# Second convolution with an fp32 first transform and its filter product kept in PSUM; layer-2 weights decoded earlier and passed through device memory

## The chip, the cores and the metric

One core of one Trainium2 chip runs the whole program. The metric is the device time of one execution in microseconds (us). Engine names in the profile: PE is TensorE (its matrix products), PEld its weight loads, DVE is VectorE, ACT is ScalarE, POOL is GpSimd, SP is the engine that issues most DMAs.

## What is computed

A spectral convolution along the sequence, then two gated layers. Cut from the reference:

```python
X = np.fft.rfft(x, axis=1)                      # x: 2 x 3008 x 256
y = np.fft.irfft(X * (filt_r + 1j * filt_i)[None], n=3008, axis=1)
x = y.reshape(6016, 256)
gate = 1.0 / (1.0 + np.exp(-(x @ w_gate)))      # layer 1, d_ff 1536; w_gate, w_val, w_out are float64
x = (gate * (x @ w_val)) @ w_out
h = x @ w_in                                    # layer 2, d_ff 2048; w_in, w_out are float64
out = (h * (1.0 / (1.0 + np.exp(-1.702 * h)))) @ w_out
```

## The kernel before, in words

**Products.** Most matrix products take operands of type fp32r. Each operand is split into a high part (an ACT copy to fp32r) and a low part (a subtraction, by `split`, L115), and `mm3` (L119 to L122) sums three products: high by high, high by low, low by high. One `mm3` is three matmuls. The layer products use a seven-product scheme on 2x2 blocks: seven `mm3` where eight would be needed.

**Stages.** The 6016 tokens are 12 tiles of 512 or 480 columns (`tiles`, six per sequence). The program runs: the convolution of sequence 0 in plain fp32 (methods `a0` to `d0`); layer 1 on tiles 0 and 1; then layer 1 on tiles 2 and 3 woven with the convolution of sequence 1 (the loop at L1004, below called the weave); layer 1 on the pairs of tiles p=2 to p=5 by the seven products (the loop at L1284); layer 2 on the pairs p=0 to p=5 (the loop at L1450). In the weave and after it the order on PE, ACT, DVE and POOL is the order in which the code emits instructions; SP's order is the emission order everywhere. Each engine works strictly through its own queue.

**The weave.** Its 20 passes k are 2 tiles by 10 blocks of 128 hidden units. In pass k the convolution unit j (16 channels, 16 units in all) is at five steps at once: `e1(k-5)`, `c1(k-1)`, `b1(k)`, `a1(k+1)`, `d1(k-2)`. `a1` splits the input into two parts (ACT, POOL); `b1` is the first transform (`mm3`) with a DVE transpose and a split; `c1` (L400) is the second transform, whose result in PSUM bank 7 is multiplied by the filter: `turn` (two ACT copies that swap real and imaginary halves into `v`; DVE `y = px * fr`, L414), `total` (DVE `v = v * fi`, L417, and `y = y + v`, L418), then the high part of `y` (ACT, L423) and its low part (DVE, L421); `d1` and `e1` are the third and fourth transforms, both in PSUM bank 6. Around them lie one pass of layer 1: two pairs of `mm3` into two of the banks 0 to 2 (`ring`), a sigmoid (L1030), the gate product on DVE (L1039), its split, and two `mm3` of an older block (`back`). In pass k the PE order is e1, c1, b1, d1, back, layer 1. `sign_f` (L278) spreads and signs the filter of one unit per pass. From k=12 on, DVE and ACT also prepare the operands of pair p=2 (`late_vec`, `late_act`).

**Layer 1, pairs.** A pass f of the loop at L1284 takes one hidden block: products x0, z1, back, y4, x5, back, back, x6, y2, back, x3 (the number is the operand's; the letter its PSUM bank). Between them DVE adds: z-add (L1360), y-add (L1369: it must read bank x before x6 adds to it), w-add (L1375: before x3 adds to it), and the gate products (L1381, L1390). `chore(n)` pops n steps of side work at four slots of a pass, whose sizes are `rate` (L1331): slot 0 lies between z-add and y-add on DVE's queue, slot 1 between y-add and w-add, slots 2 and 3 behind L1381.

**Side work.** The weights are float64 in memory: 512 KB (`load_raw`) hold a 128x512 block. `decode_steps` (L151) turns one into high and low fp32r parts: five DVE steps, two of ACT, a POOL subtraction. The 16 blocks (jobs) of layer 2 go to their final places (`slot`): five to `wl`, the rest over layer-1 weights as those are used up. Blocks 0 to 4 are decoded in p=3 and p=4, 5 to 11 in p=5, 12 to 15 in layer 2's p=0. `combine_w` (L1161) makes the four sums of two even-numbered weight blocks that the seven-product scheme needs: two in p=5, six in layer 2's p=0. Layer 2 waits in its pass fp until that pass is combined.

Of the kernel before, what the change touches and what calls it, by code (L numbers as in the profile page):

```python
# [87 lines left out]
def kernel(  # L88
# [23 lines left out]
    xscr = dram.tile([12, D, 512], F32, name="xscr")  # L112

# [104 lines left out]
    class Conv:  # L218
# [11 lines left out]
        def load_f(self, g):  # L230
            t = [self.ff.tile([P, 32, K1], F32, tag=f"f{i}", name=f"f{i}") for i in range(2)]
            gs = slice(g * 32, (g + 1) * 32)
            if self.b:
                for i in range(2):
                    nc.sync.dma_start(out=t[i][:64], in_=fd[i, :, gs])
            else:
                nc.sync.dma_start(out=t[0][:64], in_=fd[0, :, gs])
                for h in range(2):
                    hs = slice(g * 32 + h * 16, g * 32 + h * 16 + 16)
                    nc.sync.dma_start(out=t[1][h * 64:(h + 1) * 64, :16], in_=fd[1, :, hs])  # L240
            self.f[g] = t
# [158 lines left out]
        def c1(self, j):  # L400
            g, u = divmod(j, 2)
            px = ps[7][:, :384]
# [6 lines left out]
            y = self.fw.tile([P, 16, K1], F32, tag="y", name="y", bufs=1)  # L409
# [12 lines left out]

            return turn, total, lambda: nc.scalar.activation(out=yp[0], in_=y, func=AF.Copy), low  # L423
# [435 lines left out]
    sx0 = [w33.tile([P, PRE * 3, P], F32R, name=f"sx0{i}") for i in range(2)]  # L859
    pools = ExitStack()  # L860
# [11 lines left out]
    ring.remove(3)  # L872
# [121 lines left out]
    conv.sign_f(0, nc.gpsimd)  # L994
    conv.a1(0)
# [10 lines left out]
    for t in (2, 3):  # L1006
        for f in range(FK, FC1):
# [8 lines left out]
            if k + 1 < NCH:  # L1016
                conv.a1(k + 1)
# [40 lines left out]
            if k == 11:  # L1058
# [24 lines left out]
    ring.append(3)  # L1083
# [22 lines left out]
    fs.dst[3] = [packed(w, n) for w in xk]  # L1106


    def slot(j):
        if j < NWL:  # L1110
            return [w[:, j] for w in wl]
        return [w[:, j - NWL].rearrange("p v c m -> p (v c m)") for w in wg]

    NJ = FC2
    NEAR = 12
    done = set()
# [443 lines left out]
```

## Time and profile before

| | us |
|---|---|
| median of 3 runs (1247.91 to 1249.42) | 1248.92 |
| the profiled execution | 1249.48 |
| its span, first to last instruction | 1247.7 |
| PE busy in the span | 1169.2 |
| DVE, ACT, POOL busy | 762.7, 677.8, 546.8 |
| mean granted TensorE clock | 0.984 of 2.4 GHz |

A busy share is an average over stages that have different limits. In the rows, `<-` in a name stands between what is written and what is read; a bracket at the end of a row is the time that the engine sat idle before it and what ended that.

### The profile page before, as it was taken

How to read it: one execution, taken by the hardware profiler on the slowest of the kernel's cores; microseconds unless marked ns; L12 is line 12 of the kernel's file. 1: busy time of each engine (PE TensorE's matmuls, PEld its weight loads, DVE VectorE, ACT ScalarE, POOL GpSimd, SP SyncE). 2: the span in 40 equal slices, each digit the busy share in tenths (PEclk: the TensorE clock that was granted, in tenths of full speed). 3: DMA queues.
4: the chain of work that ended last, by engine and by line, in shares of the span. 5: the costliest groups of instructions: out<-in, count | busy, mean ns of one | idle time of the engine just before them, and what ended most of it. 6: DMA issues, size and time to landing. Idle time of an engine off the chain costs nothing.

```text
span 1247.7 us, 14513 instructions
## 1 busy us (share of the span) xinstructions
PE 1169.2 (94%) x4958; PEld 933.2 (75%) x4958; DVE 762.7 (61%) x1180; ACT 677.8 (54%) x1311; POOL 546.8 (44%) x426
## 2 busy tenths in 40 slices
PE   8999998787989999999998888899999999999998
PEld 4468876665767777878876675688888888888887
DVE  7899847898778876574578878742423324224211
ACT  5666526665445465454454555555655656556553
POOL 4800005665323354353353434554555545445443
PEclk9999998999989999999999999999999999999999
DMA  8564402332130011020012102001010010010000
GB/s 203 130 207 158 102 18 72 86 88 72 26 114 1 1 59 60 1 90 13 1 51 85 51 18 68 18 1 68 1 59 9 1 66 1 27 42 2 34 1 32
DMA packets 36011, 66.55 MB, mean 53 GB/s; under 512 B 3648, under 2 KB 12480, under 8 KB 35936
## 3 DMA queue, kind: packets, MB, share of 16 engines
q1 hardware_dynamic: 33968, 62.45, 17.0%
q10 hardware_dynamic: 1968, 3.17, 0.8%
q8 instruction: 39, 0.64, 0.2%
q14 instruction: 36, 0.29, 0.1%
HBM read 45.02 MB, written 19.79 MB: 52 GB/s over the span
## 4 chain that ended last, share of the span: by engine, by line
PE 50%; DVE 4%; issue 4%; POOL 2%; ACT 1%; ACTq 0%; DVEq 0%; POOLq 0%
PE ps L120 17%; PE ps L121 17%; PE ps L122 16%; DVE ps L1369 1%; DVE m L161 1%; POOL g L1415 1%; POOL wg L180 1%; DVE ps L1360 0%; POOL wo L1415 0%; DVE sg L1381 0%; DVE ex L156 0%; ACT sg L1379 0%; DVE wv L1169 0%; POOL g L117 0%; DVE yp L940 0%
## 5 line engine op out<-in xcount | busy, mean ns | idle before, releaser
L117 POOL TENSOR_TENSOR g<-sg,g 128x512 fp32r<-128x512 f32 (+1 forms) x116 | 155.7, 1350 | 269.6 <-ACT g L116 226.0
L1415 POOL TENSOR_TENSOR g<-sg,g 128x512 fp32r<-128x512 f32 (+1 forms) x128 | 167.2, 1321 | 160.7 <-ACT sg L1412 134.5
L120 PE MATMUL ps<-yp,wg 128*128 128x512 f32 (+1 forms) x373 | 147.5, 396 | 0.9 <-ACT wg L177 0.9
L121 PE MATMUL ps<-yp,wg 128*128 128x512 f32 (+1 forms) x373 | 146.3, 392 | 0.8 <-DVE yp L117 0.8
L122 PE MATMUL ps<-yp,wg 128*128 128x512 f32 (+1 forms) x373 | 145.4, 391 | 0.0
L1486 DVE TENSOR_TENSOR ps<-ps,s 128x512 f32<-128x512 f32 (+1 forms) x48 | 32.9, 686 | 153.1 <-PE ps L122 151.0
L1415 POOL TENSOR_TENSOR wo<-sg,wo 128x512 fp32r<-128x512 f32 (+1 forms) x64 | 83.1, 1307 | 83.6 <-ACT sg L1412 76.1
L1412 ACT ACTIVATE sg<-ps 128x512 f32<-128x512 f32 (+1 forms) x192 | 114.3, 595 | 0.0
L120 PE MATMUL ps<-g,wo 128*128 128x512 f32 (+1 forms) x288 | 113.1, 393 | 0.3 <-ACT wo L177 0.3
L121 PE MATMUL ps<-g,wo 128*128 128x512 f32 (+1 forms) x288 | 113.2, 393 | 0.0
L122 PE MATMUL ps<-g,wo 128*128 128x512 f32 (+1 forms) x288 | 112.9, 392 | 0.0
L116 ACT ACTIVATE g<-sg 128x512 fp32r<-128x512 f32 (+1 forms) x116 | 72.1, 622 | 70.5 <-DVE sg L1381 38.2
L1411 ACT ACTIVATE g<-ps 128x512 fp32r<-128x512 f32 (+1 forms) x128 | 76.0, 593 | 58.9 <-DVE ps L1499 58.0
L120 PE MATMUL ps<-yp,sx 128*128 128x512 f32 (+1 forms) x168 | 68.5, 408 | 25.1 <-DVE ps L1369 23.8
L120 PEld LDWEIGHTS ps<-yp,wg 128*128 128x128 f32 x373 | 71.6, 192 | 16.6 <-ACT wg L177 1.3
L121 PEld LDWEIGHTS ps<-yp,wg 128*128 128x128 f32 x373 | 71.4, 191 | 16.0 <-issue 1.7
L122 PEld LDWEIGHTS ps<-yp,wg 128*128 128x128 f32 x373 | 71.3, 191 | 14.2
L1379 ACT ACTIVATE sg<-ps 128x480 f32<-128x480 f32 (+1 forms) x48 | 28.1, 585 | 87.1 <-PE ps L122 86.8
L120 PE MATMUL ps<-g,wg 128*128 128x512 f32 (+1 forms) x192 | 74.5, 388 | 0.0
L121 PE MATMUL ps<-g,wg 128*128 128x512 f32 (+1 forms) x192 | 74.4, 388 | 0.0
L122 PE MATMUL ps<-g,wg 128*128 128x512 f32 (+1 forms) x192 | 74.3, 387 | 0.0
L1490 ACT COPY tabs<-ps 128x512 f32<-128x512 f32 (+1 forms) x48 | 27.7, 577 | 81.3 <-PE ps L122 81.3
(270 smaller groups left out, 2959.5 us busy)
## 6 DMA issues: line engine op xcount, KB each, us to landing
yraw<-xscr SPq DMA_DIRECT2D x16, 512.0 KB, 4.2
raw<-in_w_out_dram SPq DMA_DIRECT2D x14, 512.0 KB, 4.0
xscr<-yraw SPq DMA_DIRECT2D x12, 512.0 KB, 2.8
x<-in_xd_dram SPq DMA_DIRECT2D x15, 384.0 KB, 4.4
yraw<-yscr SPq DMA_DIRECT2D x11, 512.0 KB, 4.9
yscr<-tt SPq DMA_DIRECT2D x40, 128.0 KB, 2.2
f<-in_fd_dram SPq DMA_DIRECT2D x23, 192.0 KB, 4.7
raw<-in_w_in_dram SPq DMA_DIRECT2D x8, 512.0 KB, 3.7
```

The source lines that it names most:

```text
L116: nc.scalar.activation(out=dst_hi, in_=src, func=AF.Copy)
L117: lo_eng.tensor_sub(dst_lo, src, dst_hi.bitcast(F32))
L120: nc.tensor.matmul(out=o, lhsT=w[0], rhs=x[0], start=first, stop=False, **kw)
L121: nc.tensor.matmul(out=o, lhsT=w[0], rhs=x[1], start=False, stop=False, **kw)
L122: nc.tensor.matmul(out=o, lhsT=w[1], rhs=x[0], start=False, stop=last, **kw)
L161: nc.vector.tensor_scalar(m, hw, 0xFFFFF, 0x100000, op0=ALU.bitwise_and, op1=ALU.bitwise_or)
L1379: nc.scalar.activation(out=sgy, in_=y, func=AF.Sigmoid)
L1411: nc.scalar.activation(out=self.gp[0], in_=self.bank, func=AF.Gelu_apprx_sigmoid)
L1412: nc.scalar.activation(out=self.sg, in_=self.bank, func=AF.Gelu_apprx_sigmoid)
L1415: nc.gpsimd.tensor_sub(self.gp[1], self.sg, self.gp[0].bitcast(F32))
L1486: nc.vector.tensor_add(z, z, s1[:, :n])
L1490: nc.scalar.copy(s5[:, :n], y)
```

## The change

In the weave's convolution `a1` goes; `b1` multiplies the unsplit fp32 input by the unsplit fp32 table in one matmul call instead of three fp32r ones. `c1` alternates between banks 2 and 7, and its products and sum are written back into PSUM; `y` goes. Layer 1 has banks 0 and 1 only there. The filter is loaded in halves and signed and spread once for two units (`sign_g`, `spread_r`, `spread_i`). The loads of x and f move ahead in the pass. One operand of p=2 (`xk`, number 3) is split in the weave instead of at the start of p=2, and the others there move behind later products. Layer-2 blocks are decoded in p=3, p=4 and p=5 through four staging places, written to device memory (blocks 0 to 11 and the combined sums), and read back into their final places in p=5 and layer 2's p=0. The combined sums are taken from the decoded value itself (the addition of high and low part, `whole`, goes); the low part moves from POOL to DVE. Blocks 14 and 15 are left to layer 2's p=0. The slots' sizes change. In the diff, `mant`, `sign` (which also issues `raw_job(j + 2)`) and `value` are one DVE step each as before, `value` with the ACT copy of the high part; `sums(0)` and `sums(1)` are two DVE steps of 128x128 each, `sums(1)` with two ACT copies; `KEEP` is 12, and `reload_s` reads three combined sums by six DMAs.

```diff
@@ class Conv: b1, c1
-            mm3(pa, tbl3("t1"), self.st[j], True, True)
+            g, u = divmod(j, 2)
+            nc.tensor.matmul(out=pa, lhsT=tbl("t1"), rhs=self.x[g][:, u * 16:u * 16 + 16, :], start=True, stop=True)
...
-            px = ps[7][:, :384]
+            px = ps[2 if j % 2 else 7][:, :384]
...
-                nc.vector.tensor_mul(y, pxv, fr)
+                nc.vector.tensor_mul(pxv, pxv, fr)
...
                 nc.vector.tensor_mul(v, v, fi)
-                nc.vector.tensor_add(y, y, v)
+                nc.vector.tensor_add(pxv, pxv, v)
...
-                nc.vector.tensor_sub(yp[1], y, yp[0].bitcast(F32))
+                nc.vector.tensor_sub(yp[1], pxv, yp[0].bitcast(F32))
@@ the weave
-    ring.remove(3)
+    ring[:] = [0, 1]
...
-            if k + 1 < NCH:
-                conv.a1(k + 1)
...
+            if k % 2 == 1 and k // 2 + 2 < 8:
+                conv.load_x(k // 2 + 2)
+            if k and k % 2 == 0 and k // 2 + 1 < 8:
+                conv.load_f(k // 2 + 1)
...
-            if 0 < k < NCH:
-                conv.sign_f(k, nc.gpsimd)
+            if k % 2 == 1 and k // 2 + 1 < 8:
+                conv.sign_g(k // 2 + 1, nc.gpsimd)
+                conv.spread_r(k // 2 + 1)
+            if k and k % 2 == 0 and k // 2 < 8:
+                conv.spread_i(k // 2)
...
+                at_act(17, lambda: fs.hi(3))
+                at_vec(18, lambda: fs.lo(3))
@@ layer 2's weights
-    NWL = 5
+    NWL = 4
+    sp = [w34.tile([P, 3, P], F32R, name=f"sp{i}") for i in range(2)]
...
     def decode_chores(j):
...
+        hi, lo = (w[:, j % NWL] for w in wl)
...
+        def start():
...
+            nc.vector.tensor_single_scalar(ex, t["hw"], 0x7FF00000, op=ALU.bitwise_and)
...
+            nc.scalar.activation(out=t["c"], in_=ex, func=AF.Relu, bias=ebias, scale=8.0)
...
+            nc.vector.tensor_scalar(t["m"], t["hw"], 0xFFFFF, 0x100000, op0=ALU.bitwise_and, op1=ALU.bitwise_or)
...
+        def low():
+            nc.vector.tensor_sub(lo, t["f"], hi.bitcast(F32))
+            if j % 2:
+                spill()
+
+        def spill():
+            stored.add(j)
+            if j < KEEP:
+                for i, x in enumerate((hi, lo)):
+                    nc.sync.dma_start(out=wscr[j, i], in_=x.bitcast(F32))
+            if j % 2 == 0:
+                for i, x in enumerate(sp):
+                    nc.sync.dma_start(out=sscr[fp, i], in_=x.rearrange("p k m -> p (k m)").bitcast(F32))
...
+        def end():
+            r = t["r"]
+            nc.vector.tensor_sub(lo[:, P:2 * P], r[:, 0], hi[:, P:2 * P].bitcast(F32))
+            nc.vector.tensor_sub(sp[1], r[:, 1:], sp[0].bitcast(F32))
+            spill()
+
+        return [start, mant, sign, value] + ([low] if j % 2 else [lambda: sums(0), low, lambda: sums(1), end])
...
+    def reload(j):
+        for i, x in enumerate(slot(j)):
+            nc.sync.dma_start(out=x.bitcast(F32), in_=wscr[j, i])
...
+            if not chores and bulk and bulk_on[0]:
+                chores.extend(decode_chores(bulk.pop(0)))
             if chores:
                 chores.pop(0)()
@@ layer 1, pairs
+            if p == 3 and f == 0:
+                raw_job(0)
+                raw_job(1)
+            if p >= 3:
+                bulk_on[0] = f < 8 if p < 5 else bulk and bulk[0] < 14 and not chores
+            if p == 5 and f:
+                reload(f - 1)
+                if f in (5, 6):
+                    reload_s(f - 5)
+                if f == FC1 - 1:
+                    reload_s(2)
-            rate = (2, 2, 2, 2) if p == 5 else (2, 2, 1, 1) if p == 2 else (1, 2, 1, 1)
+            rate = (0, 3, 0, 2) if p in (2, 5) else (0, 3, 0, 1)
...
             if first_set:
-                fs.hi(2)
-                fs.lo(2)
             prod(x, 0, True)
@@ layer 2
-                while chores and fp not in combined:
-                    chore()
+                bulk_on[0] = True
+                if fp == 1:
+                    reload(FC1 - 1)
+                    reload_s(3)
+                if fp == 2:
+                    for q in range(4, FC2 // 2 - 1):
+                        reload_s(q)
...
-            many = 2 if p == 0 else 1
+            many = (2 if p == 0 else 1) if p or fp > 1 else 0
```

## Rows read from the trace of the kernel before

**Rows 1.** The page's first part: busy time and share of each engine.

```profile
PE 1169.2 (94%) x4958; PEld 933.2 (75%) x4958; DVE 762.7 (61%) x1180; ACT 677.8 (54%) x1311; POOL 546.8 (44%) x426
```

**Rows 2.** Stage windows: length; busy PE, PEld, DVE, ACT, POOL; granted clock, DMA, GB/s.

```profile
183.50:244.90 61.40, 51.30 (x201) 39.14 (x200) 49.79 (x62) 36.42 (x70) 34.54 (x26) 0.92 0.32 86
244.90:294.40 49.50, 42.65 (x184) 32.86 (x183) 44.71 (x57) 31.74 (x62) 33.71 (x25) 1.00 0.35 96
294.40:332.20 37.80, 28.93 (x107) 22.20 (x105) 32.90 (x48) 17.86 (x36) 18.18 (x14) 0.86 0.08 22
...
347.80:358.10 10.30, 6.67 (x22) 5.08 (x23) 8.44 (x19) 4.87 (x11) 1.36 (x1) 0.83 0.41 125
358.10:428.60 70.50, 67.56 (x296) 55.81 (x296) 57.62 (x126) 38.45 (x91) 21.22 (x17) 0.98 0.08 27
428.60:447.70 19.10, 16.38 (x74) 13.22 (x73) 14.33 (x18) 9.15 (x18) 10.08 (x8) 1.00 0.00 1
447.70:634.70 187.00, 182.16 (x791) 147.17 (x790) 117.43 (x169) 95.23 (x169) 78.30 (x62) 1.00 0.12 37
634.70:737.00 102.30, 90.10 (x395) 73.70 (x394) 82.99 (x129) 53.69 (x105) 42.14 (x32) 0.98 0.18 57
737.00:836.40 99.40, 86.99 (x347) 66.87 (x346) 71.46 (x111) 58.07 (x124) 52.08 (x40) 0.95 0.10 32
```

**Rows 3.** Waits of PE over the whole span: total us, times, longest us.

```profile
PE ps L120 <- DVE ps L1369: 23.8, 24, 2.2
PE ps L120 <- ACT g L116: 20.7, 12, 3.5
```

**Rows 4.** Timeline in one pass of the weave (k=8): start, duration, engine, line.

```profile
251.36 0.55 DVE L417 TENSOR_TENSOR v<-v,f 128x384 f32<-128x384 f32 x1
251.46 1.61 POOL L117 TENSOR_TENSOR xp<-x,xp 96x512 fp32r<-96x512 f32 x1 [1.88 <-ACT xp L116]
...
251.95 2.79 DVE L418 TENSOR_TENSOR y<-y,v 128x384 f32<-128x384 f32 x1
...
253.03 1.29 POOL L117 TENSOR_TENSOR zp<-z,zp 128x512 fp32r<-128x512 f32 x1
...
256.10 0.41 PE L120 MATMUL ps<-yp,tab 128*128 128x384 f32 x1 [0.92 <-ACT g L116]
```

**Rows 5.** Two DVE lines of the weave: duration ns min/median/max, first and last start.

```profile
L418 DVE TENSOR_TENSOR y<-y,v x16: 557/2774/2785, 192.0 to 323.5; 128x384 f32<-128x384 f32 x16
L414 DVE TENSOR_TENSOR y<-ps,f x16: 557/558/558, 189.1 to 321.8; 128x384 f32<-128x384 f32 x16
```

**Rows 6.** PE timeline of the first convolution: an fp32 first transform and its successor.

```profile
20.80 1.02 PE L309 MATMUL ps<-x,tabs 96*128 96x512 f32 x2
21.66 0.81 PE L319 MATMUL ps<-a,tabs 128*128 128x384 f32 x2
```

**Rows 7.** Timeline in one pass of layer 1, p=3 (512 columns).

```profile
465.68 0.39 PE L120 MATMUL ps<-g,wo 128*128 128x512 f32 x1
...
465.95 0.70 DVE L1369 TENSOR_TENSOR ps<-ps,tabs 128x512 f32<-128x512 f32 x1 [0.38 <-PE ps L122]
...
467.92 0.70 DVE L1375 TENSOR_TENSOR ps<-ps,tabs 128x512 f32<-128x512 f32 x1 [0.65 <-PE ps L122]
...
469.08 0.39 PE L120 MATMUL ps<-xk,wg 128*128 128x512 f32 x1
```

**Rows 8.** Timeline in one pass of layer 1, p=5 (480 columns).

```profile
661.03 1.44 DVE L161 TENSOR_SCALAR m<-raw 128x512 uint32<-128x512 uint32 x1
...
663.10 0.48 PE L120 MATMUL ps<-yp,sx 128*128 128x480 f32 x1 [1.04 <-DVE ps L1369]
...
664.52 0.37 PE L120 MATMUL ps<-g,wo 128*128 128x480 f32 x1
...
667.12 0.37 PE L120 MATMUL ps<-g,wo 128*128 128x480 f32 x1
```

**Rows 9.** The page's DMA issues: KB each, median us from issue to landing.

```profile
raw<-in_w_out_dram SPq DMA_DIRECT2D x14, 512.0 KB, 4.0
```

More of the change, by code (lines that the diff above doesn't have):

```diff
@@ L232, in load_f @@
             gs = slice(g * 32, (g + 1) * 32)
[L233 to L240, printed above, removed]
+            nc.sync.dma_start(out=t[0][:64], in_=fd[0, :, gs])
+            for h in range(2):
+                hs = slice(g * 32 + h * 16, g * 32 + h * 16 + 16)
+                nc.sync.dma_start(out=t[1][h * 64:(h + 1) * 64, :16], in_=fd[1, :, hs])
             self.f[g] = t
@@ L859 @@
     sx0 = [w33.tile([P, PRE * 3, P], F32R, name=f"sx0{i}") for i in range(2)]
+    xk = [w33.tile([P, 512], F32R, name=f"xk{i}") for i in range(2)]
     pools = ExitStack()
@@ L1105 @@
     fs.dst[2], fs.dst[6] = ([packed(h[:, c], n) for h in k26] for c in range(2))
-    fs.dst[3] = [packed(w, n) for w in xk]
+    NJ = FC2
+    KEEP = FC1
     def slot(j):
[L1110 to L1116, printed above, removed]
+        if j >= KEEP:
+            return [w[:, j - KEEP] for w in wl]
+        return [w[:, j].rearrange("p v c m -> p (v c m)") for w in wg]
     jobs2 = []
@@ L1122, in raw_job @@
     def raw_job(j):
-        src, b = jobs2[j]
-        load_raw(([w.rearrange("p (a b) -> p a b", b=b) for w in slot(j)], [src], b))
+        if j < NJ:
+            src, b = jobs2[j]
+            load_raw((None, [src], b))
     def decode_chores(j):
-        gen = decode_steps(nc.gpsimd, True)
-        def step(i):
-            if next(gen, 0) == 0:
-                done.add(j)
-            if i == 4 and j + 2 in wanted:
-                raw_job(j + 2)
-        return [lambda i=i: step(i) for i in range(7)]
+        fp = j // 2
@@ new lines, in mant, with sign, value @@
+        def mant():
+            t["f"] = t["m"].bitcast(F32)
+            nc.vector.scalar_tensor_tensor(
+                out=t["f"], in0=t["lw"], scalar=2.0**-32, in1=t["m"], op0=ALU.mult, op1=ALU.add
+            )
+        def sign():
+            cu = t["c"].bitcast(U32)
+            nc.vector.scalar_tensor_tensor(
+                out=cu, in0=t["hw"], scalar=0x80000000, in1=cu, op0=ALU.bitwise_and, op1=ALU.bitwise_or
+            )
+            raw_job(j + 2)
+        def value():
+            nc.vector.scalar_tensor_tensor(
+                out=t["f"], in0=t["f"], scalar=2.0**-20, in1=t["c"].bitcast(F32), op0=ALU.mult, op1=ALU.mult
+            )
+            nc.scalar.activation(out=hi, in_=t["f"], func=AF.Copy)
@@ L1137, in wi, with reload_s @@
+    def reload_s(fp):
+        assert 2 * fp in stored, fp
+        for k in range(3):
+            for i, x in enumerate(spare2(3 * fp + k)):
+                nc.sync.dma_start(out=x.bitcast(F32), in_=sscr[fp, i, :, k * P:(k + 1) * P])
     def wi(c, f):
@@ L1438 @@
     prev = None
+    tail = []
     for p in range(nt // 2):
@@ L1449 @@
             if p == 0:
-                if fp == 0:
-                    for q in range(2, NEAR // 2):
-                        chores.append(lazy(lambda q=q: combine_w(q)))
-                    for j in range(NEAR, NJ):
-                        chores.append(lazy(lambda j=j: decode_chores(j)))
-                        if j % 2 == 0:
-                            chores.append(lazy(lambda j=j: combine_w(j // 2)))
-                while chores and fp not in combined:
-                    chore()
-                assert fp in combined
+                bulk_on[0] = True
[5 more added lines that the diff above has]
+                        reload_s(q)
+                if not bulk and not chores and not tail:
+                    tail.append(0)
+                    reload_s(FC2 // 2 - 1)
             lhs = w_parts(fp)
@@ L1512 @@
             back()
-            chore(many + 1)
+            chore(more)
             prev = bx
```

114 lines of the change are left out of this document (39 added, 75 removed).

## Prediction, made before the changed kernel was run

> **What bounds the kernel now.** I read the page's busy shares first: PE 94%, DVE 61%, no other engine above 54% [rows 1]. So PE is the engine to save time on, but the share is a mean, and the question for this change is where PE stands still. I therefore cut the span at the starts of the passes and read each stage's busy time and granted clock [rows 2]. Against each stage I set a floor, the time of its matmuls back to back. Fifteen matmuls of 512 columns lie between the first and the last row of [rows 7], so one takes (469.08 - 465.68) / 15 = 0.227 us; twelve of 480 columns lie between the last two of [rows 8], 2.60 / 12 = 0.217 us. A layer-1 pass has 33 matmuls (seven products and four `back`, three matmuls each): 7.48 us at 512 columns, 7.15 at 480. A layer-2 pass has 45: 10.2 us.
>
> The reader is to see four stretches above their floor. The weave, 183.5 to 332.2, is 148.7 us in 17 passes. Layer 1's p=2 (347.8 to 447.7) is 99.9 against 85.8; p=5 (634.7 to 737.0) 102.3 against 85.8; layer 2's p=0 (737.0 to 836.4) 99.4 against 8 x 10.2 = 81.6, and its first pass has fewer `back` to do, so 80. Pairs p=3 and p=4 are 187.0 against 179.5, most of it at the two changes of pair. The rest of layer 2 I take as it is. Then the waits of PE [rows 3]: 23.8 us for the y-add L1369, and 20.7 us put down to an ACT copy, which in the timeline is d1's wait for bank 6 and for the low part of y, both late on DVE's queue [rows 4].
>
> **The weave.** In passes k=7 to 12 one pass takes 49.5 / 6 = 8.25 us, and DVE is busy 44.7 of 49.5 [rows 2]: DVE sets the pace. Its longest step is L418, 2.77 us in the median, where L414 with the same shape takes 0.56 [rows 5]. The timeline says why: L418 adds two SBUF tiles, and it ends only after two POOL subtractions (xp, then zp) are through, 251.46 to 254.32, while L417, which started 0.1 us before xp, took 0.55 [rows 4]. L414, which has one input in PSUM, has the same time in all 16 instances. The change makes L418 a step with a PSUM input and takes xp off POOL. I put it at 0.56 us, so DVE's pass falls from 8.25 by 2.21 to 6.04 us. An output in PSUM as well is no new case: L1369 reads and writes PSUM at 0.70 us for 512 columns [rows 7].
>
> PE's own pass is 30 matmuls, 24 of 512 columns and six of 384 (at three quarters, an estimate): 24 x 0.227 + 6 x 0.17 = 6.47 us. The fp32 transform took 21.66 - 20.80 = 0.86 us from its start to the next [rows 6] and replaces three at 0.227, so +0.18, 2.9 us over 16 units if PE is the bound. That makes 6.65. With 0.2 for hand-overs I take 6.85: PE becomes the bound, and what is late next is nothing on DVE until it has some 0.6 us more. ACT loses a copy of 0.6 us a pass; the filter's spreading stays about as long as before and is hidden. The three filter loads have a pass more to land than they need. The two banks left to layer 1 are read a pass before they are written again, so this costs nothing; if the gate product were a pass late, it would cost its 0.7 us a pass.
>
> By the Trainium skill, "FP8 and Floating Point Precision", section "TensorE Precision Notes", a true fp32 product takes four passes through the array; by that, an estimate, it would be 4 x 0.227 = 0.91 instead of 0.86 and the change 0.8 us dearer over 16 units. The row decides.
>
> Sum of the weave: k=7 to 12, 6 x 6.85 + 0.4 = 41.5 (-8.0). k=0 to 6, 61.4 us at a mean granted clock of 0.92 [rows 2], so for part of it PE ran at 1.2 GHz: six slow L418 are worth 13 us on DVE, but the tail of tiles 0 and 1 and two splits stay, so 51 (-10.5). k=13 to 16, 37.8 us at clock 0.86: L418 four times, 8.8, while DVE's preparation of p=2 stays; I take 29.5 (-8.3). The `xk` split moved in there costs +0.3. Together -26.5. Bounds: PE's floor everywhere gives -36; if half of L418's stall comes back elsewhere, -14.
>
> **Layer 1, p=2.** The old slots put two side steps between z-add and y-add; the new ones none. PE waits for the y-add in 24 passes [rows 3]. Passes 1 to 9: 70.5 against 9 x 7.15 = 64.4; I take 65.3 (-5.2). Pass 0: 10.3 at clock 0.83, with three operand splits ahead of the first adds; two are moved and one gone, 8.7 (-1.6). Passes 10 and 11: five steps a pass now just finish two blocks' sums, so the four sums for p=3 are done in one burst at pass 10, +0.8. Sum -6.0; between -10 and -2.
>
> **p=3 and p=4.** Here the decoding goes from 5 blocks to 11, four steps a pass, three of them in slot 1. That slot has room from the y-add's end to where the w-add must be done: PE reaches x3 469.08 - 465.95 = 3.13 us after the y-add starts, less 0.6 and 0.7 for the two adds and 0.1 for the hand-over, 1.7 us. Three steps of 0.62 are 1.9, and where a low part follows its ACT copy within the slot DVE waits some 0.7 for ACT. Going through the 13 steps of a pair of blocks four by four I get stalls of 0 to 1.0 us a pass: 2.2 us in p=3 and 4.5 in p=4, against about 2.5 in these pairs before. Sum +4.2; between 0 and +9.
>
> **p=5.** Before, eight steps a pass with POOL's low parts among them; a mask step took 1.44 us instead of 0.42 and PE waited 1.04 behind it [rows 8]. Now three blocks are left, done by pass 3, and the layer-2 operands by pass 10. Floor 85.8 plus 2.9 of slot stalls, 88.7 (-13.6); between -16 and -9. The reloads are DMAs behind passes that are over; no engine waits for them before layer 2.
>
> **Layer 2, p=0.** Six sums and four blocks become two blocks from pass 2 on. 80 plus 1.6 gives 81.6 (-17.8); between -19 and -12, the latter if a reloaded block comes a pass late.
>
> **The sum.** -26.5 - 6.0 + 4.2 - 13.6 - 17.8 = -59.7. The profiled execution took 1249.5 (span 1247.7 and 1.8 around it), 0.6 above the median; 1249.5 - 59.7 = 1189.8, as a median 1189. With every part at its better or its worse bound the sum would be -81 or -28; that all fall on one side together is unlikely.
>
> **The rivals.** *L417 takes L418's place.* `v * fi` still has two SBUF inputs and starts only 0.1 us ahead of a POOL step [rows 4]. If at the new pace it comes behind zp and the filter's sign step, it stands 1.3 to 2.6 us, and the weave is DVE-bound again: 16 units at 1.0 us net, 1205. For it: the small margin. Against: xp, the step that was closest, is gone, and zp starts after L417's operands are ready. The Trainium skill, "SBUF — State Buffer", section "Who interferes with whom", says the same of any DVE step with two SBUF inputs against a POOL step that reads SBUF, whoever comes first; [rows 4] agree. *Slot 1 is too small.* If the three steps cost twice the stalls that I counted, p=3 to p=5 lose another 10: 1199. *PE at its floor nearly everywhere:* half of what is left above the floors goes, 1176. *The in-place product does not come free of POOL* (the change does not do what it says): the weave gains only xp's share, some 5 us, 1211. *Slower:* SP issues spills, raw loads and reloads in one order. If a spill or a reload that waits holds up the raw loads, DVE stands at a block's first step with the y-add and w-add behind it. A load takes 4.0 us to land [rows 9]; 16 of them fully in view are 64 us, 1253. It decides once a load is issued less than 4 us ahead of its first step; by the code it is issued some eight steps, two passes or 15 us, ahead.
>
> **How the numbers follow.** My forecast 1189 has 0.58; L417 0.10; slot 1 0.12; PE's floor 0.12; in-place 0.05; slower 0.03. For 8 in 10 the range takes in the floor case, slot 1, L417 and nearly the in-place case: 1173 to 1210. About 0.2%, 2.5 us, is what a measurement of this kernel can tell from no change. All but one case lie well below: faster 0.96, same 0.01, slower 0.03.
>
> **What would show it.** After: L418 at 0.56 us in all 16 instances; passes k=7 to 12 at about 6.9 us with PE and not DVE full; the y-add's wait nearly gone and a smaller wait for the w-add (L1375's place) in p=3 and p=4; p=5 near 89 us; layer 2's p=0 near 82. The forecast is wrong if L417 stretches, if DVE waits for raw loads, or if layer 2 waits for a reloaded block.

## The result, and the profile after

The changed kernel takes 1211.0 us (median of 4 runs, 1210.7 to 1213.6) against 1249.2 beside it: a ratio of 0.970, interval 0.968 to 0.972. The gain is 38 us where 60 were forecast, and 1211.0 lies 1 us outside the range. The profiled execution took 1210.7, its span 1208.9.

The page's first part, then the stages, cut at the starts of the passes as in [rows 2] (columns as there):

```profile
PE 1161.1 (96%) x4942; PEld 921.4 (76%) x4942; DVE 705.9 (58%) x1172; ACT 671.3 (56%) x1279; POOL 481.1 (40%) x386
```

```profile
183.60:233.70 50.10, 47.39 (x191) 34.38 (x190) 35.84 (x62) 34.16 (x62) 20.53 (x16) 1.00 0.36 105
233.70:276.00 42.30, 42.30 (x178) 31.81 (x177) 31.91 (x58) 30.00 (x56) 19.43 (x16) 1.00 0.38 113
276.00:308.80 32.80, 27.21 (x106) 20.05 (x105) 27.61 (x48) 16.82 (x34) 12.60 (x10) 0.95 0.10 24
...
334.00:403.60 69.60, 68.03 (x296) 54.12 (x296) 58.26 (x126) 37.49 (x90) 21.02 (x18) 1.00 0.08 28
403.60:425.20 21.60, 17.89 (x73) 14.49 (x72) 15.34 (x21) 9.13 (x18) 9.40 (x8) 0.92 0.00 0
...
622.60:714.00 91.40, 87.18 (x392) 72.30 (x391) 61.71 (x99) 48.00 (x91) 29.11 (x25) 1.00 0.39 127
714.00:797.60 83.60, 80.75 (x347) 65.49 (x346) 40.32 (x55) 51.14 (x97) 44.68 (x36) 0.98 0.19 60
```

The second stage (k=7 to 12) has changed its bound: PE is busy 42.30 of 42.30 us and DVE 31.91, where it was 42.65 and 44.71 of 49.50 [rows 2]. The row from 334.0 to 403.6, p=2's passes 1 to 9, looks full as well (PE 68.0 of 69.6), yet it is only 0.9 us shorter than before. A stage's length tells more than PE's busy share, because a matmul that starts late is drawn longer.

PE's waits over the whole span, then the two steps of the weave that the forecast turned on (duration in ns: least, median, most; first and last start):

```profile
PE ps L122 <- DVE ps L1395: 12.2, 22, 2.4
PE ps L122 <- DVE ps L1387: 9.2, 8, 2.5
PE ps L122 <- ACT g L118: 6.1, 5, 2.0
```

```profile
L402 DVE TENSOR_TENSOR ps<-ps,v x16: 566/566/567, 192.1 to 300.2; 128x384 f32<-128x384 f32 x16
```

```profile
L401 DVE TENSOR_TENSOR v<-v,f x16: 517/552/555, 191.5 to 299.7; 128x384 f32<-128x384 f32 x16
```

The sum (L402, L418 before) is down from 2774 to 566 ns in all 16 instances and `v * fi` (L401, L417 before) keeps its 0.55. The y-add's wait (L1387) falls from 23.8 to 9.2 us [rows 3], but the w-add (L1395), which was not among the large waits, now has 12.2.

Stage lengths in us: the weave from its first sigmoid to its last, every other stage from the start of its first pass to the start of the next stage's. The last columns are experiments, of which the next section tells:

| stage | before | after | forecast | e2 | e3 | e6 | e7 | e8 | e9 | e12 | e13 |
|---|---|---|---|---|---|---|---|---|---|---|---|
| weave, k=0 to 19 | 158.4 | 135.0 | 131.9 | 138.1 | 136.3 | 144.6 | 135.5 | 136.5 | 135.5 | 136.5 | 134.9 |
| p=2 | 99.9 | 100.8 | 93.9 | 100.4 | 93.7 | 100.6 | 97.5 | 100.9 | 100.8 | 92.3 | 92.6 |
| p=3 | 94.7 | 97.9 | 191.3 | 97.9 | 97.8 | 97.6 | 97.9 | 97.9 | 95.2 | 95.2 | 95.1 |
| p=4 | 92.4 | 99.5 | (both) | 99.5 | 99.4 | 99.5 | 99.5 | 99.5 | 97.6 | 96.4 | 95.1 |
| p=5 | 102.3 | 91.3 | 88.7 | 91.3 | 91.3 | 91.7 | 91.3 | 91.3 | 90.9 | 90.9 | 92.2 |
| layer 2, p=0 | 99.4 | 83.6 | 81.6 | 84.0 | 82.0 | 83.4 | 83.7 | 79.9 | 83.4 | 79.9 | 79.9 |
| span | 1247.7 | 1208.9 | 1188.0 | 1212.7 | 1201.4 | 1218.2 | 1206.1 | 1206.3 | 1206.1 | 1191.7 | 1190.6 |

What follows on layer 2's p=0 is 411.3 us in both kernels, so the whole miss lies in this table: 3.1 in the weave, 6.9 in p=2, 6.1 in p=3 and p=4, 2.6 in p=5 and 2.0 in layer 2's p=0, 20.7 of the 20.9 us between the spans. A stage that an edit does not touch moves by up to 1.6 us from run to run (the weave: 134.9 to 136.5), so the kernels that ran once (e2, e4 and e7 to e10) are read by the stage that their edit touches.

### The profile page after: what moved, and what is told of

It is laid out like the page before. It is cut to its first block, busy times and chain, and to the rows that moved or that the text cites. A ratio compares the mean times of both kernels' runs of the same rounds, so it can differ in the third digit from the quotient of the medians.

```text
span 1208.9 us, 14593 instructions
## 1 busy us (share of the span) xinstructions
PE 1161.1 (96%) x4942; PEld 921.4 (76%) x4942; DVE 705.9 (58%) x1172; ACT 671.3 (56%) x1279; POOL 481.1 (40%) x386
## 4 chain that ended last, share of the span: by engine, by line
PE 73%; DVE 15%; ACT 6%; issue 5%; POOL 1%; DMA 0%; DVEq 0%; ACTq 0%; SPq 0%; POOLq 0%
PE ps L122 24%; PE ps L123 23%; PE ps L124 23%; DVE ps L1387 1%; DVE ps L1395 1%; ACT g L118 1%; DVE sg L1401 1%; ACT tabs L1381 1%; DVE sx L894 1%; DVE sg L1410 1%; DVE m L1133 1%; DVE sg L1030 1%; DVE ex L1125 1%; DVE m L1145 1%; DVE wl L1151 1%
## 5 line engine op out<-in xcount | busy, mean ns | idle before, releaser
L119 POOL TENSOR_TENSOR g<-sg,g 128x512 fp32r<-128x512 f32 (+1 forms) x116 | 146.4, 1265 | 347.7 <-ACT g L118 346.1
L1435 POOL TENSOR_TENSOR g<-sg,g 128x512 fp32r<-128x512 f32 (+1 forms) x128 | 165.7, 1311 | 157.1 <-ACT sg L1432 139.2
L122 PE MATMUL ps<-yp,wg 128*128 128x512 f32 (+1 forms) x382 | 150.2, 394 | 0.8 <-ACT wg L179 0.8
L123 PE MATMUL ps<-yp,wg 128*128 128x512 f32 (+1 forms) x382 | 148.8, 390 | 0.8 <-DVE yp L119 0.8
L124 PE MATMUL ps<-yp,wg 128*128 128x512 f32 (+1 forms) x382 | 148.1, 388 | 0.0
L1435 POOL TENSOR_TENSOR wo<-sg,wo 128x512 fp32r<-128x512 f32 (+1 forms) x64 | 83.4, 1314 | 78.5 <-ACT sg L1432 71.0
L122 PE MATMUL ps<-g,wo 128*128 128x512 f32 (+1 forms) x288 | 112.1, 389 | 0.3 <-ACT wo L179 0.3
L123 PE MATMUL ps<-g,wo 128*128 128x512 f32 (+1 forms) x288 | 111.6, 388 | 0.0
L124 PE MATMUL ps<-g,wo 128*128 128x512 f32 (+1 forms) x288 | 111.5, 388 | 0.0
L122 PEld LDWEIGHTS ps<-yp,wg 128*128 128x128 f32 x382 | 72.4, 189 | 16.8 <-ACT wg L179 1.2
L123 PEld LDWEIGHTS ps<-yp,wg 128*128 128x128 f32 x382 | 72.3, 189 | 16.4 <-issue 1.9
L124 PEld LDWEIGHTS ps<-yp,wg 128*128 128x128 f32 x382 | 72.2, 189 | 14.4
L122 PE MATMUL ps<-yp,sx 128*128 128x512 f32 (+1 forms) x168 | 67.5, 402 | 10.9 <-DVE ps L1387 9.2
L124 PE MATMUL ps<-yp,sx 128*128 128x512 f32 (+1 forms) x168 | 65.0, 387 | 0.0
```

What stands on the lines that cost most here:

```text
L119: lo_eng.tensor_sub(dst_lo, src, dst_hi.bitcast(F32))
L122: nc.tensor.matmul(out=o, lhsT=w[0], rhs=x[0], start=first, stop=False, **kw)
L123: nc.tensor.matmul(out=o, lhsT=w[0], rhs=x[1], start=False, stop=False, **kw)
L124: nc.tensor.matmul(out=o, lhsT=w[1], rhs=x[0], start=False, stop=last, **kw)
L1435: nc.gpsimd.tensor_sub(self.gp[1], self.sg, self.gp[0].bitcast(F32))
```

## The experiments

**Do the parts add?** The kernel before with only the weave's edits (unsplit first transform, product and sum in PSUM, filter for two units, two banks), nothing of the decoding:

```diff
-            mm3(pa, tbl3("t1"), self.st[j], True, True)
+            g, u = divmod(j, 2)
+            nc.tensor.matmul(out=pa, lhsT=tbl("t1"), rhs=self.x[g][:, u * 16:u * 16 + 16, :], start=True, stop=True)
...
-                nc.vector.tensor_add(y, y, v)
+                nc.vector.tensor_add(pxv, pxv, v)
```

> The kernel before with the weave's change alone (unsplit fp32 first transform, filter product kept in PSUM, two banks, filter spread for two units); the layer-2 weights, the slots and the split of xk stay as before. Theory: the parts of the change add, so the weave (from the first to the last sigmoid of the weave, 158.4 us before, 134.9 in the changed kernel) takes 134 to 136 and the whole about 1249.2 - 23.5 = 1225.7; p=2 to layer 2 stay at their lengths of before (99.9, 187.0, 102.3, 99.4). Rival: the weave was gained at the cost of what comes behind it (p=2's 100.8 us are due to the weave's earlier end or its left-over work); then p=2 grows here too, by 5 us or more over 99.9.

Measured: 1228.7 us, ratio 0.983 (0.981 to 0.984). Its weave is 134.9, p=2 99.8, p=3 and p=4 94.9 and 93.4, p=5 104.2, layer 2's p=0 99.7. The weave's gain is there in full without the rest, and the stages behind it stay near the kernel before (p=5, 1.9 us longer, moves most). The parts add, and the misses can be looked for stage by stage.

**The weave: what was worth how much?** First the sum is put back into SBUF, all else as in after:

```diff
-                nc.vector.tensor_mul(pxv, pxv, fr)
+                nc.vector.tensor_mul(y, pxv, fr)
...
-                nc.vector.tensor_add(pxv, pxv, v)
+                nc.vector.tensor_add(y, y, v)
```

> The changed kernel, but the filter's products are summed in SBUF again (tile y), all else as changed. Theory: the sum escapes POOL because one input lies in PSUM; in SBUF it starts just after zp's subtraction on POOL and takes 1.5 to 2.5 us instead of 0.57, DVE paces the weave again at about 7.8 to 8.2 us a pass where the changed kernel has 7.05, weave 146 to 152. Rival: taking xp off POOL was enough; the sum stays below 0.8 us and the weave within 1 us of 134.9.

Then the sum stays in PSUM and the first transform is split again:

```diff
+        def a1(self, j):
...
+            xp = self.pair([XR, 16, 32], "xp")
+            split(*xp, x, nc.gpsimd)
...
-            g, u = divmod(j, 2)
-            nc.tensor.matmul(out=pa, lhsT=tbl("t1"), rhs=self.x[g][:, u * 16:u * 16 + 16, :], start=True, stop=True)
+            mm3(pa, tbl3("t1"), self.st[j], True, True)
```

> The changed kernel with the weave's first transform split again (ACT copy, POOL subtraction, three fp32r products), the filter sum kept in PSUM. Theory: PE bounds the weave, the three products are 0.17 us a unit cheaper than the fp32 one, and the sum does not meet POOL, so the weave is 132 to 135 (134.9 as changed), no longer. Rival: what was gained came from taking xp off ACT and POOL; then v * fi, which has two SBUF inputs and starts 0.1 us from xp, stretches over 0.8 us and the weave goes to 140 or more.

The sum of e2 by line; `y` is read and written in SBUF:

```profile
L403 DVE TENSOR_TENSOR y<-y,v x16: 557/1532/1544, 192.8 to 304.0; 128x384 f32<-128x384 f32 x16
```

With `xp` gone from POOL, the sum in SBUF takes 1.53 us instead of 2.77: the trace has one POOL subtraction to get past instead of two. The weave takes 138.1, 3.1 more than after, and 1.6 to 3.2 more than in the other runs that have after's weave. Splitting the first transform instead costs 9.6 (144.6; median of the kernel 1220.2, ratio 0.976, 0.973 to 0.978), although its sum stays at 0.57 us. I had expected it the other way round: most of the gain from the sum. Neither alone comes near the 158.4 of before: together they make 12.7 of the 23.4 us that lie between the kernels, and no run tells whether the rest is what the two do together or belongs to the filter's spreading and the banks. In e6 neither DVE step stretches; its timeline shows ACT's queue instead: the copy of `xp` and three copies that spread the filter stand ahead of the sigmoid (247.05), whose gate product on DVE, after 1.64 us of waiting, holds up e1's transpose and the low part that d1 needs:

```profile
247.05 0.60 ACT L1030 ACTIVATE sg<-ps 128x512 f32<-128x512 f32 x1
...
247.68 0.69 DVE L1039 TENSOR_TENSOR sg<-ps,sg 128x512 f32<-128x512 f32 x1 [1.64 <-ACT sg L1030]
```

So I moved only `a1`, behind the sigmoid and the sum's high part:

```diff
-            if k + 1 < NCH:
-                conv.a1(k + 1)
...
             high_y()
+            if k + 1 < NCH:
+                conv.a1(k + 1)
```

> The kernel of the run with the first transform split again (weave of 144.6 us), with one thing moved: the ACT copy of the input's high part and POOL's subtraction for its low part are issued behind the unit's sigmoid and the sum's high part, not ahead of them. Theory (ACT's in-order queue: the input's copy and the three spread copies hold up the sigmoid, so the gate product on DVE, so the transpose of e1 and the low part that d1 waits for): the weave falls most of the way back, to 135.5 to 139.5 us, and PE's idle time put down to ACT in 200 to 320 us falls from 12.9 us to under 6. Rival (it is the work itself: two more matmuls a chunk at 0.28 us and POOL's 1.04 us a chunk, wherever they stand): 142 to 145 us. Two more matmul passes a chunk alone are some 16 x 0.75 = 12 us of PE less the 0.86 of fp32 each, so PE can't be behind by itself.

PE's waits in the weave, first of e6, then of e10:

```profile
PE ps L122 <- ACT g L118: 12.9, 10, 2.9
```

```profile
PE ps L123 <- POOL xp L119: 8.9, 11, 0.9
PE ps L122 <- ACT g L118: 2.9, 2, 2.1
PE ps L122 <- ACT xp L118: 2.7, 3, 1.5
```

The waits put down to ACT fall from 12.9 to 5.6, as the theory said, but the weave only to 140.9, between the two expectations: with the copy later, the low part of `xp` on POOL is late, 8.9 us in 11 waits. Both places are too tight. I read it that what the unsplit transform buys in the weave is less PE's or DVE's work than a step of ACT and one of POOL that had no good place in the pass; with two places run, and the second one between the expectations, that the work itself has a part in it is not ruled out.

**p=2: why no gain?** Two kernels change only how many side steps stand in the four slots of its passes, (0,3,0,2) in after: one moves a step of slot 3 to slot 0, the other one of slot 1 to slot 0.

```diff
-            rate = (0, 3, 0, 2) if p in (2, 5) else (0, 3, 0, 1)
+            rate = (1, 3, 0, 1) if p == 2 else (0, 3, 0, 2) if p == 5 else (0, 3, 0, 1)
```

> The changed kernel with p=2's slots at 1, 3, 0, 1 instead of 0, 3, 0, 2 (still five steps a pass, now one between z-add and y-add and one in place of two ahead of the older gate product). Theory: passes 1 to 9 take 7.81 us because the last low parts wait for ACT in slot 3, meet POOL's subtraction (1.41 instead of 0.49 us), push the gate product and ACT's copy behind it and so the y-add and the w-add; without that they take 7.15 to 7.3, p=2 95 to 96.5 instead of 100.8, the whole -4 to -6 us. Rival: three steps in slot 1 are too many whatever comes ahead; then the w-add's wait stays at 0.1 to 0.2 us a pass and the passes at 7.5 or more.

In the second the new tuple is (1, 2, 0, 2):

> The changed kernel with p=2's slots at 1, 2, 0, 2: two steps are left in slot 3, slot 1 has one less. Theory (slot 3's collision with POOL is the cause): the y-add stays late by 0.1 us or more, now with a step ahead of it, passes 7.3 to 7.6; the low parts stay at 1.4 us. Rival (three steps in slot 1): the w-add's wait goes and the passes fall to 7.2 or less.

One pass of after in the timeline (start, duration; a bracket is the idle time before the row and its releaser):

```profile
356.54 1.22 POOL L119 TENSOR_TENSOR g<-sg,g 128x480 fp32r<-128x480 f32 x1 [3.67 <-ACT g L118]
356.70 1.41 DVE L894 TENSOR_TENSOR sx<-wr,sx 128x128 fp32r<-128x128 f32 x2 [0.47 <-ACT sx L891]
...
358.03 0.65 DVE L1410 TENSOR_TENSOR sg<-ps,sg 128x480 f32<-128x480 f32 x1
...
358.71 0.60 ACT L118 ACTIVATE g<-sg 128x480 fp32r<-128x480 f32 x1 [1.39 <-DVE sg L1410]
...
359.23 0.55 ACT L1381 COPY tabs<-ps 128x480 f32<-128x480 f32 x1
...
359.80 0.67 DVE L1387 TENSOR_TENSOR ps<-ps,tabs 128x480 f32<-128x480 f32 x1 [0.55 <-ACT tabs L1381]
...
360.20 0.38 PE L124 MATMUL ps<-g,wo 128*128 128x480 f32 x1
...
360.52 0.19 PEld L122 LDWEIGHTS ps<-yp,sx 128*128 128x128 f32 x1 [0.35 <-DVE ps L1387]
360.52 0.49 PE L122 MATMUL ps<-yp,sx 128*128 128x480 f32 x1
...
360.85 0.38 PE L123 MATMUL ps<-yp,sx 128*128 128x480 f32 x1
...
362.37 0.38 PE L124 MATMUL ps<-g,wo 128*128 128x480 f32 x1
...
362.92 0.49 PE L122 MATMUL ps<-xk,wg 128*128 128x480 f32 x1 [0.17 <-DVE ps L1395]
...
363.24 0.38 PE L123 MATMUL ps<-xk,wg 128*128 128x480 f32 x1
```

The same part of a pass in e3:

```profile
357.92 1.74 DVE L877 TENSOR_TENSOR wv<-wg,wg 128x512 f32<-128x512 f32 x1
...
358.63 0.56 ACT L1381 COPY tabs<-ps 128x480 f32<-128x480 f32 x1 [0.88 <-PE ps L124]
...
359.59 0.65 DVE L1387 TENSOR_TENSOR ps<-ps,tabs 128x480 f32<-128x480 f32 x1
...
362.14 0.37 PE L124 MATMUL ps<-g,wo 128*128 128x480 f32 x1
...
362.35 0.38 PE L122 MATMUL ps<-xk,wg 128*128 128x480 f32 x1
```

Read the pass of after from the top. Slot 3's last two low parts (L894) wait for their ACT copies and start 0.16 us after POOL's subtraction: 1.41 us for the two, where one takes 0.28 in e3. The older gate product (L1410) comes late behind them, so ACT makes its high part late, and ACT's next step, the copy for the y-add (L1381), is late too. The y-add waits for it, and the three steps of slot 1 behind it push the w-add. On PE, x6 starts 0.32 us after its predecessor instead of 0.217, the next matmul again 0.33 after that; x3 starts after 0.55 and its successor after 0.32. The four excesses are 0.10 + 0.11 + 0.33 + 0.10 = 0.64 us, nearly the whole difference of a pass (7.81 in the median) to its floor (7.15). PE's list of waits shows only 0.17 of them, since its weight load does the waiting (0.35 us in the PEld row) and the matmul with it is drawn longer.

In e3 the x3 starts after 0.21 us, a pass takes 7.24 and p=2 93.7, 7.1 less: 1203.2 us, ratio 0.963 (0.961 to 0.964). Passes 1 to 9 give 4.2 of the 7.1; 2.3 come from passes 10 and 11, where the burst described below stops PE for 1.75 us instead of 2.47 and the granted clock stays at 1.00. The step now in slot 0 even takes longer there, 1.74 us behind POOL, and costs little, because that slot has room. In e4, with slot 1 lighter but slot 3 as it was, a pass takes 7.63 and p=2 98.2. So it was slot 3 for the larger part: e4 gains 0.18 us a pass, e3 0.57. That a DVE step with two SBUF inputs stands behind a POOL step that reads SBUF and was issued before it is the rule of the Trainium skill, "SBUF — State Buffer", section "Who interferes with whom"; the rows at 356.54 and 356.70 agree, and the step of e3 too.

**p=2, passes 10 and 11.** Only the place of the four sums for p=3 changes, from the end of pass 9's steps to pass 10's slots:

```diff
-                if f == 9:
+                if f == (10 if p == 2 else 9):
```

> The changed kernel, but in p=2 the four sums for p=3 are put on the list in pass 10 instead of pass 9, so that they go through the slots of pass 10 and not in one burst at its start. Theory: the burst delays the y-add of pass 10 by 2.5 us and costs a stretch at the lower TensorE clock; passes 10 and 11 fall from 21.6 to 17.5 to 18.5. Rival: pass 11 with its operand splits sets the end, and they stay at 20.5 or more.

In after the four sums stand in one burst, at 404.88 to 407.5; below its first, the y-add behind it, the matmul that waits, and the stage windows at that place:

```profile
404.88 0.68 DVE L934 TENSOR_TENSOR xs<-yraw 128x512 f32<-128x512 f32 x1
...
409.17 0.67 DVE L1387 TENSOR_TENSOR ps<-ps,tabs 128x480 f32<-128x480 f32 x1 [0.55 <-ACT tabs L1381]
...
409.89 0.77 PE L122 MATMUL ps<-yp,sx 128*128 128x480 f32 x1 [2.47 <-DVE ps L1387]
...
410.46 0.60 PE L123 MATMUL ps<-yp,sx 128*128 128x480 f32 x1
```

```profile
409.80:413.30 3.50, 3.41 (x9) 2.91 (x10) 0.70 (x2) 0.54 (x1) 0.24 (x1) 0.52 0.00 0
413.30:416.00 2.70, 2.70 (x14) 2.33 (x13) 1.63 (x3) 1.61 (x5) 1.23 (x1) 1.00 0.00 0
```

PE stands for 2.47 us, and the clock granted in the 3.5 us behind it is 0.52, so nearly all of it is at the 1.2 GHz level: six matmuls in a row start 0.40 us apart instead of 0.217, some 1.1 us on top. In e7 the two passes take 18.3 instead of 21.6.

**p=3 to p=5: the slots.** The steps of slot 1 go from three to two and one stands in slot 0:

```diff
-            rate = (0, 3, 0, 2) if p in (2, 5) else (0, 3, 0, 1)
+            rate = (0, 3, 0, 2) if p == 2 else (1, 2, 0, 2) if p == 5 else (1, 2, 0, 1)
```

> The changed kernel with the slots of p=3 and p=4 at 1, 2, 0, 1 and of p=5 at 1, 2, 0, 2 (as many steps a pass, one of them moved from behind the y-add to ahead of it); p=2 stays at 0, 3, 0, 2. Theory: three full-size steps in slot 1 hold the w-add up and PE waits for it; with two they fit, p=3 falls from 97.9 to 95.5 to 96.5, p=4 from 99.5 to 95.5 to 97, p=5 from 91.3 to 90, the whole -5 to -7 us. Rival: eleven blocks in 16 passes are simply more DVE work than these passes hold, whichever slot they lie in; then the wait goes over to the y-add and the three pairs stay within 2 us of 288.7 together.

Three executions took 1202.2 to 1206.7 us, ratio 0.964 (0.961 to 0.967); the fourth, the profiled one, took 5007 us, so the stages come from a second run of the same kernel:

> The kernel after, with only the steps per slot of the passes p=3, 4 and 5 changed from (0,3,0,1), (0,3,0,1), (0,3,0,2) to (1,2,0,1), (1,2,0,1), (1,2,0,2). Its first profiled execution (the same kernel, timed at 0.9636 of the kernel before) was disturbed throughout, so this run is for the stage lengths alone. After's p=3, 4, 5 take 97.9, 99.5, 91.3 us. Theory (three steps in slot 1 push the w-add behind the next hand-over, 0.1 to 1.3 us a pass, and each stalled hand-over costs the next matmul 0.1 us more): p=3 95.0 to 96.5, p=4 95.5 to 97.0, p=5 90.0 to 91.0, everything else as in after; span 1202 to 1205. Rival (the loss of p=3 and p=4 lies in the first passes of the pair, where the evacuation's copies and the first steps meet, not in the slots): p=3 and p=4 come down by 0.5 us each at most, span 1207 to 1208.5.

p=3 is 95.2 and p=5 90.9, where the theory put them; p=4 is 97.6, 0.6 above it, and the span, 1206.1, 1.1 above it. The w-add's waits in p=3 and p=4 go from 5.7 to 0.7 us, while the y-add's go from 4.2 to 5.9, nearly all in the first and last passes of the two pairs; the longest is in p=4's first:

```profile
527.98 0.50 PE L122 MATMUL ps<-yp,sx 128*128 128x512 f32 x1 [2.14 <-DVE ps L1387]
```

The granted clock in the 4.0 us behind it is 0.64. In e12 below the same wait (2.12 us) has a clock of 1.00 behind it, and p=4 takes 96.4, inside the theory.

**Layer 2, p=0: the last two blocks spread.** One step instead of two, and two instead of three, in the slots of p=0 ("block row 0" below):

```diff
-            many = (2 if p == 0 else 1) if p or fp > 1 else 0
+            many = 1 if p or fp > 1 else 0
```

> The changed kernel with one step a slot (two in the later ones) in layer 2's p=0, as in its other pairs, instead of two and three. Theory: the steps at the end of a pass put ACT's copy of a block's high part ahead of ACT's copy of bank x, PE waits 2.3 us in pass 3 and then runs 2 us at the lower clock; spread out, p=0 falls from 83.6 to 79.5 to 81. Rival: the waits belong to blocks 14 and 15 wherever their steps lie; 83 or more.

In after the copy that feeds the z-add stands behind a decode step on ACT and PE waits; the row by itself has the granted clock behind it:

```profile
745.97 0.63 ACT L1148 ACTIVATE wl<-m 128x512 fp32r<-128x512 f32 x1 [0.70 <-DVE m L1145]
...
746.50 0.57 ACT L1498 COPY s<-ps 128x512 f32<-128x512 f32 x1
...
747.12 0.50 PE L122 MATMUL ps<-sx,wo 128*128 128x512 f32 x1 [2.34 <-ACT s L1498]
```

```profile
747.00:751.00 4.00, 3.88 (x10) 3.11 (x11) 1.92 (x3) 1.65 (x4) 1.34 (x2) 0.59 0.04 11
```

It is pass 10 of p=2 again: a stall of over 2 us, then about 3.5 us near the lower clock level. Spread, the stage takes 79.9 us (-3.7).

The stall and the slower clock can be told apart, because e3 has after's layer 2 and the same stall with the full clock behind it:

```profile
741.23 0.50 PE L122 MATMUL ps<-sx,wo 128*128 128x512 f32 x1 [2.33 <-ACT s L1498]
```

```profile
741.00:745.00 4.00, 3.77 (x17) 3.13 (x18) 2.72 (x5) 1.75 (x4) 1.45 (x2) 1.00 0.06 17
```

There the stage takes 82.0, so of the 3.7 us about 2.1 are the stall and 1.6 the clock. A stall of this length is not always followed by the slower clock.

**All four at once.** Do the gains add? The first attempt has e3's, e9's and e7's edits and one decode step in every slot of layer 2's block row 0:

```diff
-            more = many + 1 if many else 0
+            more = many + 1 if p else many
```

> The kernel after with the four placements that the single runs point to, and nothing else: one step more in slot 0 and one less in slot 3 in p=2 (1,3,0,1); (1,2,0,1) in p=3 and p=4 and (1,2,0,2) in p=5; the four sums of p=2 in pass 10 instead of pass 9; in layer 2 one decode step a slot in block row 0 instead of two. If the gains add (single runs, stage by stage: p=2 f0 to f9 -4.8, f10 and f11 -3.3, p=3 and p=4 -4.0 by estimate, p=5 -0.5 by estimate, layer 2 p=0 -3.7): 1211.0 - 16.3 = 1194.7 us, 1192 to 1198. If they overlap (a step moved out of one late place makes the next one late): 1199 to 1203. The weave, 135.0, and everything from layer 2's second block row on stay as they are.

1192.6 us, ratio 0.952 (0.951 to 0.954), but it leaves out one reload: the code issues that of the last pair's sums only in a pass that starts with no side steps left, and with so few steps a slot none does. The second attempt has e8's slots and leaves nothing out:

> The same four placements as the run before, but in layer 2's block row 0 only the slots that had two decode steps get one and the slots that had three get two (as in the single run of that edit); with one step in every slot the last decode ended so late that the condition for the reload of the last pair's sums was never met, so the run before left that reload out. Theory (the gains add): that run's stages, weave 135.5, p=2 92.4, p=3 95.2, p=4 96.7, p=5 90.9, with layer 2 p=0 at 79.9 of the single run instead of 78.5: 1194 us, 1191 to 1197. Rival (the gain was the reload left out and the decode that came late): layer 2 p=0 back at 83 to 84 and a median of 1197 to 1200.

1193.4 us (1193.0 to 1195.2), ratio 0.955 (0.953 to 0.957), inside the theory's range. The column e12 stands where the single runs put each stage, except that p=2 gains 8.5 where e3 and e7 have 7.1 and 3.3, since both of them shorten passes 10 and 11. The forecast's 93.9 for p=2 is beaten (92.3), p=3 and p=4 come to 191.6 (forecast 191.3) and layer 2's p=0 to 79.9 (81.6): these sizes could be had with the same work, but not in the order in which the change does it.

**The first passes of p=3 to p=5.** On top of e12, the steps of slots 0 and 1 go out of them:

```diff
+            if p > 2 and f == 0:
+                rate = (0, 0, 0, 2)
```

> The run beside it, with no decode step in slots 0 and 1 of the first pass of p=3, 4 and 5 (two in slot 3 instead), where the evacuation's copies of the pair before also stand on DVE and ACT. In the run with (1,2,0,1) the waits left there were y-add 1.0 and w-add 0.5 us (p=3), y-add 2.1 (p=4), y-add 1.05 and w-add 0.6 (p=5). Theory (copies and steps meet): with the steps gone, p=3 94 to 95, p=4 94.5 to 95.7, p=5 89.0 to 90.2, together 3 to 5 us less than the run beside it, whose p=3 to p=5 are expected at 95.2, 96.7, 90.9. Rival (the copies alone make the y-add late, and the decode's steps only move to later passes): p=3 to p=5 within 1.2 us of the run beside it.

1192.5 us (1191.4 to 1193.3): 1.0 less than e12, with overlapping ranges. p=4 gains 1.3, p=5 loses 1.3, since its passes 3 to 8 get longer, and p=3 stays. The y-add's wait in the first pass of p=4 halves, from 2.14 us in e9 to 1.03, but those of p=3 and p=5 stay at 1.0. The three pairs together take 282.4 us against 282.5, as the rival's number had it, but the cause that both expectations named, the evacuation's copies, does not fit the first pass of p=4:

```profile
512.16 1.36 DVE L928 TENSOR_TENSOR xk<-xs,xk 128x512 fp32r<-128x512 f32 x1 [1.22 <-ACT xk L923]
...
514.15 0.63 ACT L118 ACTIVATE g<-sg 128x512 fp32r<-128x512 f32 x1 [1.55 <-DVE sg L1412]
...
515.29 0.70 DVE L1389 TENSOR_TENSOR ps<-ps,tabs 128x512 f32<-128x512 f32 x1 [0.57 <-ACT tabs L1383]
...
515.90 0.68 DVE L1267 COPY yraw<-ps 128x512 f32<-128x512 f32 x1
...
516.04 0.50 PE L122 MATMUL ps<-yp,sx 128*128 128x512 f32 x1 [1.03 <-DVE ps L1389]
```

The evacuation's DVE copy (L1267) starts at 515.90, after the y-add. What is late is the same chain as in p=2's passes: here the low part of the next pair's last operand stands on DVE for 1.36 us beside POOL, then come the gate product, ACT's high part, ACT's copy for the y-add, the y-add. That reading rests on the timeline; no run took that low part away.

## Why the prediction was half right

The forecast was 22 us too low. None of the three signs by which it said that it would be wrong came (`v * fi` did not stretch, DVE did not wait for a raw load, layer 2 did not wait for a reload); most of what went wrong lies in the hand-overs of layer 1, which none of them watched.

**The weave: mechanism right, 3.1 us too much.** The sum is at 0.57 us, PE is the bound, DVE has room; k=0 to 6 came to 50.1 (forecast 51) and k=7 to 12 to 42.3 (41.5). The term that was too good is k=13 to 16, 32.8 instead of 29.5: DVE is busy 27.6 of 32.8 there and PE 27.2, at a granted clock of 0.95, and three waits of PE, 5.2 us in all, are left while DVE prepares p=2. The weights inside the term were wrong, though. I gave the gain to the sum's 2.21 us on DVE and took the unsplit transform for a small extra cost on PE. e2 and e6 show that the transform matters more: without it the weave loses 9.6 us, without the PSUM sum 3.1. The rivals on this term did not come: `v * fi` stayed at 0.55 us, and the in-place product is free of POOL. That the in-place rival's number was 1211 too is chance: it had the weave gain some 5 us, and the weave gained 23.4.

**p=2: the step that failed.** The prediction took 5.2 us off passes 1 to 9 because no step stands between z-add and y-add any more; they gave 0.9. No step stands there, and the y-add still is late, because it waits for an ACT copy that stands behind a gate product which slot 3 makes late; e3, with that slot lighter, takes 4.2 us off these passes. The prediction looked at the slots between z-add and w-add and counted slots 2 and 3 as free: nothing there was priced against POOL, nor followed round through ACT. The waits of [rows 3] did move; they went to the w-add. And the burst of pass 10 was put at +0.8, where it makes 3.3, as e7 shows: the stall and the slower clock behind it. Pass 0 took 9.6 us for 8.7: PE stands 2.41 us there for the w-add, with a granted clock of 0.51 in the 3.5 us behind it. In e4, with two steps in slot 1, the wait is 1.69 us, the clock stays at 1.00, and the pass takes 8.0.

```profile
331.18 0.72 PE L122 MATMUL ps<-xk,wg 128*128 128x480 f32 x1 [2.41 <-DVE ps L1395]
```

**p=3 and p=4: right side, undersized.** +4.2 was forecast, +10.3 measured (187.1 to 197.4), just above the upper end of 9. The mechanism, three steps are too much for slot 1, was the right one and its rival case (slot 1 too small, doubled stalls) the one that came: e9 takes 4.6 us back with the slot alone. Of the 10.3, 3.2 are the first passes of the two pairs (19.5 us, 16.3 before), which the forecast did not price by themselves; e9 leaves them at 19.5. I had not counted that each late hand-over also delays the matmul after it by 0.1 us.

**p=5 and layer 2's p=0: nearly right.** -11.0 for -13.6, and -15.8 for -17.8. In p=5 PE waits 2.7 us for the w-add and 1.2 for the y-add; the chore-free passes run at their floor, 7.15. In layer 2 the excess is one stall and the slower clock behind it, which e8 removes. No engine waited for a reload or a raw load, so the slower rival has nothing in the trace.

**The sum.** The misses fell on one side because most of them have one cause: e12 changes nothing but the place of side steps, and its span is 17.2 us shorter. I had reckoned every slot by itself, from a trace in which those steps stood elsewhere. The forecast said that all parts falling on one side was unlikely; with a common cause it is not. e12, 1193, shows that all but some 4 us of the forecast can be had from this work by its placement; e12's weave and p=5 are still 4.6 and 2.2 us above the forecast, its p=2 and layer 2's p=0 1.6 and 1.7 below.

## What to carry to other kernels

To place side steps between hand-overs, follow each step round the whole loop: what it waits for, which POOL step it will meet, which engine's in-order queue its lateness passes to, and which hand-over that engine feeds next. A slot far from the hand-over can hurt more than one ahead of it, and a step that is slower in one slot may cost nothing there; so try placements one at a time and read the lengths of the stage's passes, not the list of waits. Do not let side work gather into a burst that stops PE: in pass 10 of p=2 and in layer 2 the slower clock behind stalls of 2.47 and 2.34 us cost some 1.1 and 1.6 us more.

## What the runs showed of the chip that I had not expected

- A late hand-over costs PE more than its idle time: behind a matmul that started late, the next one started 0.32 to 0.33 us after it, instead of 0.217 (rows at 360.52 and 362.92), also where the listed idle time was only 0.17 us or none.
- After stalls of 2.34 and 2.47 us the granted clock was 0.59 for 4.0 us and 0.52 for 3.5 us, with PE busy nearly all that time. It is not so after every such stall: in e3 it was 1.00 after 2.33 us, in e12 after 2.12 us, while in e9 it was 0.64 after 2.14 us at the place where e12 had 1.00. In layer 2's p=0 that alone made 1.6 us.
- A 128x384 DVE sum with both inputs in SBUF took 2.77 us where two POOL subtractions overlapped it, 1.53 where one did, and 0.57 with one input in PSUM.
